# Sliding-window attention and a SwiGLU block on one core: the order of the first loads, and where two-chunk blocks begin

## Chip, cores, metric

The kernel runs on one core of one Trainium2 chip. The metric is device microseconds (us) of one execution. The median of three runs before the change is 333.36 us (332.61 to 333.39).

## What is computed

Attention with a causal window of 64 positions over 8 batches, 8 heads, 576 positions and head size 64, and then a gated feed-forward over all 4608 tokens:

```python
scores = scale * np.matmul(q, k.transpose(0, 1, 3, 2))
mask = (rel >= 0) & (rel < window)                 # rel = query - key, window = 64
attn = softmax(np.where(mask, scores, -1e9))
x = np.matmul(attn, v)                             # tokens x 512 after the heads are joined
g = x @ w_gate
val = x @ w_val
out = (g * sigmoid(g) * val) @ w_out               # 512 -> 1536 -> 512
```

All inputs and the output are float32 in memory; the kernel computes in bfloat16 and accumulates in float32.

## The kernel before

**Tiling.** The 4608 tokens are 36 chunks of 128; four chunks are one feed-forward group of 512, so there are nine groups. A chunk goes through four steps. Its q and k are laid out transposed (qT, kT). `Sb` or `Sk` (L412, L442) makes the scores on PE, and ACT takes their exponential into pt. `AVs`, `AVmm` or `AVp` (L536, L496, L568) multiplies pt with V on PE, and DVE divides by the sum (`AVn`, `AVpn`), which gives xb. `X` (L654) transposes xb into xT, on PE with a copy by ACT or DVE, or by a DMA transpose on the SP queue. A group's feed-forward is `F` (L713): for one or two of the twelve 128-wide slices f, eight or sixteen matmuls with Wg and Wv (L733), a tanh on ACT (L739) and two DVE operations (L741, L743) that write hT; then `O` (L749) multiplies a chunk's hT with Wo in twelve matmuls (L759), ACT copies the result and issues the store.

**Order.** Everything is recorded in one hand-written order in `build` (L848), and each engine runs its own operations in that order; waits come from the reads and writes named with each operation (`_Graph`, L31). A DMA is issued by the engine whose queue it is recorded on: nearly all loads by POOL (`load`, `load2`, `load_w`, `load_wo`), transposes by SP, stores by ACT. So POOL does nothing further while its next operation waits. POOL's DMAs also use 16 semaphores in turn: the seventeenth waits for the first.

**The first four chunks** go a path of their own. `first_loads` fetches k of chunks 0 and 1 in float32, a DVE cast (L685, shown as L242) makes bfloat16 of it, and `first_T` transposes it on PE (L692). `T2` (L355) transposes k or q of two chunks on PE in sixteen small transposes (L368) with two copies, each on ACT or DVE; its source buffers ks2 and qs2 hold two stages of two chunks in turn. `Sbias` (L398) adds the mask as a large negative number with one matmul per bank (L406), from nmask, which DVE computes out of mask. `AVs` (L546) needs, beside V of its own chunk, a copy of V shifted by 64 rows, vs, which `shift` (L530) makes on DVE or POOL from two neighbouring chunks of V. `warm` (L700) issues matmuls on zeros, "dummies", whose result nobody reads.

**Later chunks.** From chunk 8 on, `load` brings q and k into rings of six buffers (kn, qn), and `T` (L345) transposes them by DMA on SP. `B(n)` (L641) does the attention of chunk n, with the scores of chunk n+1 between its two halves. From chunk P0 on `P(n)` (L626) does the attention of chunks n and n+1 as one block, with the scores of n+2 and n+3 between its halves; the loop over u (L960) calls it on even u behind an `O`. `kt` and `qt` (L376, L379) say up to which chunk the transposes are issued at n; they step up one chunk at P0 - 1.

The loads before the first feed-forward, in POOL's order (L798): q of chunks 0 and 1, k and q of chunks 2 and 3, identity and mask, V0, V1, Wg slices 0-1, V2, V3, Wv 0-1, Wg 2-3, the first shifted copy, Wv 2-3, both weights 4-5, three shifted copies, weights 6-9. V of a chunk is 128 KB in bfloat16, two slices of one weight 256 KB, a `load2` of k or q 256 KB, Wo 1536 KB in two halves.

Of the kernel before, what the change touches and what calls it, by code (L numbers as in the profile page):

```python
# [5 lines left out]
ALU = mybir.AluOpType  # L6
# [145 lines left out]
class _Kernel:  # L152
# [7 lines left out]
    NO = 4  # L160
    NST = 4
    KC = 18
    P0 = 20

    def __init__(self, nc, q, k, v, wg, wv, wo, out):
        self.nc, self.q, self.k, self.v = nc, q, k, v
# [98 lines left out]
            out=m[:, :], in_=m[:, :], compare_op=ALU.not_equal, fill=1.0, base=0,  # L265
            pattern=[[-1, 128]], channel_multiplier=1), writes=["ident"])

    def init_mask(self, part):
        g = self.g
        mm = self.mask[:, :].rearrange("p (v e q) -> p v e q", v=3, e=2)  # L270

        def sel(e_, cmp, fill, base, cm, step):
            a = mm[:, :, e_, :]
            g.op("pool", lambda e: e.affine_select(
                out=a, in_=a, compare_op=cmp, fill=fill, base=base,
                pattern=[[0, 3], [step, 64]], channel_multiplier=cm), writes=["mask"])

        if part == 0:
            sel(0, ALU.is_ge, 0.0, 0, -1, 1)
            sel(0, ALU.is_ge, 1.0, 64, -1, 1)  # L280
            return
        sel(1, ALU.is_gt, 0.0, 0, 1, -1)
        sel(1, ALU.is_ge, 0.0, 64, -1, 1)
        g.op("pool", lambda e: e.memset(mm[64:128, 1, 0, :], 0.0), writes=["mask"])
        g.op("pool", lambda e: e.memset(mm[0:64, 2, 1, :], 0.0), writes=["mask"])

    def init_nmask(self):
        self.g.op("dve", lambda e: e.tensor_scalar(
# [66 lines left out]
    def T2(self, st, x, engs):  # L355
        g = self.g
        src = (self.ks2 if x == "k" else self.qs2)[st % 2]
        dst = self.kT if x == "k" else self.qT
        z0 = (2 * st) % self.NZ
        for cc in range(2):  # L360
            bank, bk = self.bank("a")
            tb = bank[:, 0:256].bitcast(BF).rearrange("p (c j t) -> p c j t", c=2, j=2)

            def pe(e, cc=cc, tb=tb):
                for c in range(2):
                    for j in range(2):
                        for p in range(2):
                            r = e.transpose(tb[64 * p:64 * p + 64, c, j, :], src[:, 4 * cc + 2 * c + p, j, :], self.ident[:, :])  # L368
                return r

            g.op("pe", pe, reads=["ident", ("s2", x, st % 2, 0), ("s2", x, st % 2, 1)], writes=[bk])
            d = dst[:, 2 * cc:2 * cc + 2, 128 * z0:128 * z0 + 256].rearrange("p c (t j) -> p c t j", j=2)
            a = tb.rearrange("p c j t -> p c t j")
            self.copy(engs[cc], d, a, [bk], [(x + "T", z, cc) for z in (z0, z0 + 1)])

    def kt(self, n):  # L376
        return n + 3 + (n >= self.P0 - 1)

# [151 lines left out]
    def shift(self, n, r, eng):  # L530
        i = n + r - 1
        src, dst = self.va[n], self.vs[i]
        rows = slice(64 * r, 64 * r + 64)
        self.copy(eng, dst[rows, :, 0:64], src[rows, :, 0:64], [("va", n), ("va", n, 0), ("va", n, 1)], [("vs", i, r)])

    def AVs(self, st):  # L536
        n, bx, av, done = st
# [97 lines left out]
    def AV(self, n):  # L635
        st = self.AVa(n)
        self.AVmm(st, 0)
        self.AVmm(st, 1)
        self.AVn(st)
# [109 lines left out]
    def O(self, c, u):  # L749
        g = self.g  # L750
        ih = c % self.NH
        hT = self.hT[ih]
        io = (4 * c + u) % self.NO
        ost = self.ost[io]
        OB, ok = self.bank("f")

        def pe(e):
            for f in range(NF):
                r = e.matmul(OB[:, :], hT[:, f, 128 * u:128 * u + 128], self.Wo[:, f, :],  # L759
                             start=(f == 0), stop=(f == NF - 1))  # L760
            return r

        g.op("pe", pe, reads=self.hTk(ih) + [("Wo", f) for f in range(NF)], writes=[ok])
        g.op("act", lambda e: e.activation(ost[:, :], OB[:, :], ACTF.Copy), reads=[ok], writes=[("ost", io)])  # L764
        r0 = 512 * c + 128 * u
        g.op("act", lambda e: e.dma_start(self.out[r0:r0 + 128, :], ost[:, :]), reads=[("ost", io)], dma=True)
# [31 lines left out]
    def loads(self):  # L798
        self.first_loads()
        self.load2(0, "q")  # L800
        self.load2(1, "k")
        self.load2(1, "q")
        self.init()
        self.init_ident()
        self.init_mask(0)
        self.init_mask(1)
        self.load(0, "v")
        self.load(1, "v")
        self.load_w("g", 0, 2)
        self.load(2, "v")  # L810
        self.load(3, "v")
        self.load_w("v", 0, 2)
        self.load_w("g", 2, 4)
        self.shift(1, 1, "pool")
        self.load_w("v", 2, 4)
        self.W(4, 6)
        self.shift(2, 0, "pool")
        self.shift(2, 1, "pool")
        self.shift(3, 0, "pool")
        for a in range(6, 10, 2):  # L820
            self.W(a, a + 2)

    def early_loads(self):
        self.load2(2, "k")
        self.load2(2, "q")
        self.W(10, 12)
        self.load(4, "v")
        self.load(5, "v")

    def more_loads(self):  # L830
        self.load2(3, "k")
        self.load2(3, "q")
        self.load(6, "v")
        self.load(7, "v")
        self.load(8, "kq")
        self.load_wo(0, 6)
        self.load_wo(6, 12)
        self.load(9, "kq")
        self.load(10, "kq")
        self.load(8, "v")  # L840
        self.load(11, "kq")
        self.load(9, "v")
# [5 lines left out]
    def build(self):  # L848
        F, S, AV, X, T2, O = self.F, self.S, self.AV, self.X, self.T2, self.O
        self.loads()  # L850
        self.banks("a", [4, 5, 6, 7, 0, 1, 2, 3, 4, 5, 0, 1, 2, 3, 0, 1, 6, 7, 4, 5, 6, 7, 4, 5, 2, 3, 6, 7])
        self.warm(48, n=112)
        self.first_T(("dve", "act"))
        self.init_nmask()
        self.warm(2)
        s0 = self.Sa(0)
        T2(0, "q", ("act", "dve"))
        self.Sbias(s0)
        self.Sb(s0)
        T2(1, "k", ("dve", "dve"))  # L860
        s1 = self.Sa(1, True)
        self.Sb(s1)
        T2(1, "q", ("dve", "act"))
        self.early_loads()
        s2, s3 = self.Sa(2, True), self.Sa(3)
        a0, a1, a2, a3 = self.AVa(0), self.AVa(1), self.AVa(2), self.AVa(3)
        self.AVs(a0)
        self.shift(0, 1, "dve")
        self.shift(1, 0, "dve")
        self.AVn(a0)  # L870
        self.Sb(s2)
        self.AVs(a1)
        self.AVn(a1)
        self.Sbias(s3)
        X(0, "act", "a")
        self.Sb(s3)
        X(1, "dve", "a")
        self.warm(3, j=2)
        self.AVs(a2)
        self.AVn(a2)  # L880
        self.warm(2, j=2)
        self.AVs(a3)
        self.AVn(a3)
        F(0, (0, 1), 0, 256)
# [10 lines left out]
        F(0, (6,))  # L895
        T2(2, "k", ("act", "act"))
        T2(2, "q", ("act", "act"))
        F(0, (7,))
        S(4)
        F(0, (8,))  # L900
# [1 line left out]
        F(0, (9,))  # L902
        X(4, "act")
        T2(3, "k", ("act", "act"))
        F(0, (10,))
        a5 = self.AVa(5)
        self.AVmm(a5, 0)
        T2(3, "q", ("act", "act"))
        self.AVmm(a5, 1)
        self.AVn(a5)  # L910
        F(0, (11,))
        X(5, "act")
        F(1, (0, 1), 0, 128)
        S(6)
        F(1, (0, 1), 128, 256)
        F(1, (2, 3), 0, 256)
        self.B(6)
        F(1, (4, 5), 0, 256)
        X(6, "act")
        F(1, (6, 7), 0, 256)  # L920
        AV(7)
        self.load(12, "kq")
        self.load(10, "v")
        for n in range(8, 12):
            self.Tkq(n)
        O(0, 0)
        X(7, "act")
# [16 lines left out]
        X(9)  # L944
        self.Tkq(14)
        F(1, (9,))
        O(0, 2)
        F(1, (10,))
        self.B(10)
        F(1, (4, 5), 256, 512)  # L950
        F(1, (11,))
        X(10, "act")
        self.B(11)
        O(0, 3)
        X(11, "act")
        F(1, (6, 7), 256, 512)
        lk, lq = max(15, self.kt(12)), max(15, self.qt(12))
        tk, tq = 14, 14
        for c in range(2, NFC):
            for u in range(4):  # L960
                n = 4 * c + u + 4
# [90 lines left out]
```

## Time and profile before

| | us |
|---|---|
| median of three runs | 333.36 (332.61 to 333.39) |
| the profiled execution | 333.81 |
| its span, first to last instruction | 331.8 |
| PE busy | 322.5 (97%) |
| DVE busy | 202.3 (61%) |
| ACT busy | 136.0 (41%) |
| POOL busy, mostly with issuing loads | 108.5 (33%) |
| feed-forward matmuls L733, with Wg and with Wv | 111.4 + 111.2 |
| output matmuls L759 | 95.9 |

Times within the profile are us from the start of the span. A line number is that of the helper that records the operation, so all feed-forward matmuls share L733, and all copies of one helper share L242 (DVE, POOL) or L240 (ACT). The duration shown for a matmul includes the tail in which the next one already runs; what one costs in a row is the distance of the starts. An entry in brackets gives the idle time of the engine ahead of the instruction and what ended it. The chain of waits is followed back from the last instruction, at each step to what released it.

### The profile page before, as it was taken

To read this page: it belongs to the slowest core of one execution; us is meant where nothing else is said; L and a number is where in the kernel's file an instruction comes from. 1 tells how busy PE (TensorE), PEld (TensorE's weight loads), DVE (VectorE), ACT (ScalarE), POOL (GpSimd) and SP (SyncE) were. 2 spreads that over 40 slices of the span, in tenths; PEclk is the share of its full clock that TensorE was granted. 3 is DMA by queue.
4 is the path that set the end of the run, shared out by engine and by line. 5 is a ranking of instruction groups with operands and counts; after the bars stand their busy time and mean duration, and the time that the engine had idled before them with its cause. 6 is when DMAs were issued, how large, how long until landed. Compare 5 with 4: busy or idle time off the path is not lost.

```text
span 331.8 us, 8107 instructions
## 1 busy us (share of the span) xinstructions
PE 322.5 (97%) x3459; PEld 167.9 (51%) x3459; DVE 202.3 (61%) x350; ACT 136.0 (41%) x242; POOL 108.5 (33%) x140
## 2 busy tenths in 40 slices
PE   6789999989999999999999999999999999999996
PEld 5466577646544444444545454545454544444444
DVE  4658777558666666665565656565656566555510
ACT  2643763535444544444525252434343432332221
POOL 8899974353623533334542424100000000000000
PEclk9999999999999999999999999999999999999999
DMA  9999999999999999999999999961412111100012
GB/s 143 153 187 188 170 181 151 153 171 148 173 174 175 169 163 120 119 131 171 167 137 132 141 111 130 118 106 52 108 49 63 49 49 47 49 32 33 34 63 95
DMA packets 161572, 39.86 MB, mean 120 GB/s; under 512 B 148608, under 2 KB 157056, under 8 KB 161536
## 3 DMA queue, kind: packets, MB, share of 16 engines
q0 software_dynamic: 111056, 18.62, 76.4%
q1 hardware_dynamic: 45024, 11.15, 25.0%
q10 hardware_dynamic: 5456, 9.57, 8.9%
q8 instruction: 27, 0.44, 0.5%
q14 instruction: 9, 0.07, 0.1%
HBM read 37.75 MB, written 9.44 MB: 142 GB/s over the span
## 4 chain that ended last, share of the span: by engine, by line
PE 78%; DMA 10%; POOL 8%; SPq 1%; issue 1%; ACT 0%; DVE 0%; ACTq 0%; POOLq 0%
PE ps L733 46%; PE ps L759 26%; DMA kn<-in_k_dram 6%; DMA qT<-qn 3%; DMA va<-in_v_dram 2%; PE ps L594 2%; POOL va L319 1%; SPq L352 1%; POOL qs L328 1%; PE ps L519 1%; POOL Wv L334 1%; PE ps L462 1%; POOL ks L328 1%; POOL Wg L334 1%; PE ps L781 1%; POOL vs L242 1%
## 5 line engine op out<-in xcount | busy, mean ns | idle before, releaser
L741 DVE SCALAR_TENSOR_TENSOR uu<-sig,ps 128x512 bf16<-128x512 bf16 (+1 forms) x109 | 74.0, 679 | 71.3 <-ACT sig L739 71.3
L733 PE MATMUL ps<-xT,Wg 128*128 128x512 bf16 (+2 forms) x488 | 111.4, 355 | 0.0
L733 PE MATMUL ps<-xT,Wv 128*128 128x512 bf16 (+2 forms) x488 | 111.2, 355 | 0.0
L759 PE MATMUL ps<-Wo,hT 128*128 128x512 bf16 x420 | 95.9, 379 | 0.0
L739 ACT ACTIVATE sig<-ps 128x512 bf16<-128x512 f32 (+1 forms) x109 | 64.9, 596 | 69.1 <-PE ps L733 68.7
L743 DVE SCALAR_TENSOR_TENSOR hT<-uu,ps 128x512 bf16<-128x512 bf16 (+1 forms) x109 | 74.3, 682 | 3.8
L733 PEld LDWEIGHTS ps<-xT,Wv 128*128 128x128 bf16 x488 | 47.1, 98 | 46.4
L733 PEld LDWEIGHTS ps<-xT,Wg 128*128 128x128 bf16 x488 | 44.7, 98 | 41.9
L759 PEld LDWEIGHTS ps<-Wo,hT 128*128 128x128 bf16 x420 | 40.9, 98 | 49.0
L764 ACT ACTIVATE ost<-ps 128x512 f32<-128x512 f32 x35 | 20.9, 597 | 94.9 <-PE ps L759 94.9
L319 POOL DMA_DIRECT2D kn<-in_k_dram x31 | 27.5, 900 | 59.0 <-DMA kT<-kn 57.9
L319 POOL DMA_DIRECT2D va<-in_v_dram x40 | 35.0, 890 | 11.2 <-PE ps L594 5.9
L319 POOL DMA_DIRECT2D qn<-in_q_dram x31 | 27.6, 892 | 30.5 <-DMA qT<-qn 29.9
L438 ACT ACTIVATE pt<-ps 128x512 bf16<-128x512 f32 x36 | 19.5, 595 | 9.8 <-PE ps L430 9.8
L474 ACT ACTIVATE pt<-ps 128x512 bf16<-128x512 f32 x36 | 18.8, 601 | 5.1 <-PE ps L466 4.7
L621 DVE RECIPROCAL rp<-ps 128x14 f32<-128x14 f32 (+1 forms) x16 | 3.2, 203 | 20.5 <-PE ps L594 20.5
L482 DVE TENSOR_TENSOR pt<-pt,kmask 128x1024 bf16<-128x1024 bf16 x18 | 12.3, 684 | 3.5 <-ACT pt L474 3.5
L565 DVE TENSOR_TENSOR xb<-ps,rc 128x512 bf16<-128x512 f32 x20 | 13.8, 692 | 0.7
L482 DVE TENSOR_TENSOR pt<-pt,mask 128x1024 bf16<-128x1024 bf16 x14 | 9.6, 684 | 4.7 <-ACT pt L438 4.6
L623 DVE TENSOR_TENSOR xb<-ps,rp 128x896 bf16<-128x896 f32 (+1 forms) x16 | 11.1, 691 | 0.6
L519 PE MATMUL ps<-va,pt 64*64 64x65 bf16 x504 | 10.2, 197 | 0.1
L519 PEld LDWEIGHTS ps<-va,pt 64*64 64x64 bf16 x504 | 6.8, 106 | 5.9 <-issue 4.0
(63 smaller groups left out, 152.0 us busy)
## 6 DMA issues: line engine op xcount, KB each, us to landing
out_dram<-ost ACTq DMA_DIRECT2D x35, 256.0 KB, 3.4
va<-in_v_dram POOLq DMA_DIRECT2D x32, 128.0 KB, 7.0
kn<-in_k_dram POOLq DMA_DIRECT2D x25, 128.0 KB, 9.5
qn<-in_q_dram POOLq DMA_DIRECT2D x25, 128.0 KB, 9.5
Wg<-in_moe_w_gate_dram POOLq DMA_DIRECT2D x6, 256.0 KB, 6.5
Wv<-in_moe_w_val_dram POOLq DMA_DIRECT2D x6, 256.0 KB, 6.7
Wo<-in_moe_w_out_dram POOLq DMA_DIRECT2D x2, 768.0 KB, 16.0
qs<-in_q_dram POOLq DMA_DIRECT2D x3, 256.0 KB, 6.5
```

The lines of the kernel that those rows point to most:

```text
L319: self.g.op("pool", lambda e, d=d, a=a: e.dma_start(d, a), writes=ks, dma=True)
L438: g.op("act", lambda e, po=po, p=p: e.activation(po, sv[p], ACTF.Exp, scale=SCALE), reads=[bx[p][1]], writes=[pk[p]])
L474: g.op("act", lambda e, po=po, p=p: e.activation(po, sv[p], ACTF.Exp, scale=SCALE), reads=[bx[p][1]], writes=[pk[p]])
L482: self.g.op("dve", lambda e: e.tensor_tensor(pt, pt, m, ALU.mult), reads=pk + [key], writes=pk)
L519: x = e.matmul(av[64 * c:64 * c + 64, p, j, :], pp[rows, h, 64 * a:64 * a + 64], vv[rows, h, 0:65], start=first, stop=phase == 1, skip_gro ...
L565: g.op("dve", lambda e: e.tensor_tensor(xo, av[:, :, :, 0:64], rb, ALU.mult), reads=bk + [("rc", ir)], writes=[("xb", ix, 0), ("xb", ix, 1)])
L733: r = e.matmul(bank[:, a * n:a * n + n], W[:, kk, f * 128:f * 128 + 128], xT[:, kk, lo:hi], start=(kk == 0), stop=(kk == NK - 1))
L739: g.op("act", lambda e, G=bank: e.activation(sig[:, 0:w], G[:, 0:w], ACTF.Tanh, scale=0.5), reads=[bk], writes=[("sig", i)])
L741: g.op("dve", lambda e: e.scalar_tensor_tensor(uu[:, 0:w], sig[:, 0:w], 1.0, G[:, 0:w], ALU.add, ALU.mult), reads=[("sig", i), gk], writes ...
L743: g.op("dve", lambda e: e.scalar_tensor_tensor(out, v3(uu), 0.5, v3(V), ALU.mult, ALU.mult), reads=[("uu", i), vk], writes=[("hT", ih, f) ...
L759: r = e.matmul(OB[:, :], hT[:, f, 128 * u:128 * u + 128], self.Wo[:, f, :], start=(f == 0), stop=(f == NF - 1))
L764: g.op("act", lambda e: e.activation(ost[:, :], OB[:, :], ACTF.Copy), reads=[ok], writes=[("ost", io)])
```

## The change

- The mask: POOL makes one half with two selects; DVE makes the other half as one minus the first and clears two corners. nmask follows at once, ahead of `first_T`.
- POOL's order: V0 to V3 directly behind the mask, then Wg and Wv 0-1, Wg 2-3, the first shifted copy (chunk 0, moved from DVE to POOL), Wv 2-3, Wg 4-5, four shifted copies, Wv 4-5, weights 6-7. Weights 8-9 now follow k and q of chunks 4 and 5.
- The scores of chunk 1 come ahead of `T2` of chunks 2 and 3; one copy of `T2(1, "k")` and the copy of X(0) change engines; the bias of chunk 2 is added later. Dummies: 44 of 132 columns instead of 48 of 112 at the start, and three of 512 columns instead of seven afterwards, at other places.
- k and q of chunks 8 and 9 come by `load2(4)`, in `late_loads` behind `T2` of chunks 4 and 5, and are transposed on PE by two more `T2`; the four DMA transposes go. Wo follows `load2(4)`.
- Groups 0 and 1: the attention of chunk 5 is no longer split around `T2(3, "q")`, that of chunk 7 is split around `T2(4, "q")`; F(1, (0, 1)) is one piece of 256 columns instead of two of 128; O(0, 2), F(1, (11,)), X(11) and O(0, 3) move by a step.
- P0 is 16 instead of 20: blocks of two chunks from chunk 16.

```diff
-    P0 = 20
+    P0 = 16
...
-    def init_mask(self, part):
+    def init_mask(self):
...
+        a, b = mm[:, :, 0, :], mm[:, :, 1, :]
+        for fill, base in ((0.0, 0), (1.0, 64)):
+            g.op("pool", lambda e, fill=fill, base=base: e.affine_select(
+                out=a, in_=a, compare_op=ALU.is_ge, fill=fill, base=base,
+                pattern=[[0, 3], [1, 64]], channel_multiplier=-1), writes=["mask"])
+        src = mm[:, 0:1, 0, :].to_broadcast([128, 3, 64])
+        one = g.op("dve", lambda e: e.tensor_scalar(b, src, -1.0, 1.0, ALU.mult, ALU.add), reads=["mask"], writes=["mask"])
+        g.op("dve", lambda e: e.memset(mm[64:128, 1, 0, :], 0.0), writes=["mask"])
+        g.op("dve", lambda e: e.memset(mm[0:64, 2, 1, :], 0.0), writes=["mask"], after=one)
...
+        rd = [("va", n), ("va", n, 0), ("va", n, 1)] + (["mask"] if eng == "pool" else [])
+        self.copy(eng, dst[rows, :, 0:64], src[rows, :, 0:64], rd, [("vs", i, r)])
...
+        self.init_mask()
+        self.init_nmask()
+        for n in range(4):
+            self.load(n, "v")
+        self.W(0, 2)
         self.load_w("g", 2, 4)
+        self.shift(0, 1, "pool")
+        self.load_w("v", 2, 4)
+        self.load_w("g", 4, 6)
         self.shift(1, 1, "pool")
-        self.load_w("v", 2, 4)
-        self.W(4, 6)
         self.shift(2, 0, "pool")
         self.shift(2, 1, "pool")
         self.shift(3, 0, "pool")
-        for a in range(6, 10, 2):
-            self.W(a, a + 2)
+        self.load_w("v", 4, 6)
+        self.W(6, 8)
...
         self.load2(2, "q")
+        self.W(8, 10)
         self.W(10, 12)
...
-        self.load(8, "kq")
+
+    def late_loads(self):
+        self.load2(4, "k")
+        self.load2(4, "q")
         self.load_wo(0, 6)
         self.load_wo(6, 12)
-        self.load(9, "kq")
...
-        self.warm(48, n=112)
+        self.warm(44, n=132)
         self.first_T(("dve", "act"))
-        self.init_nmask()
-        self.warm(2)
         s0 = self.Sa(0)
         T2(0, "q", ("act", "dve"))
         self.Sbias(s0)
+        self.warm(2)
         self.Sb(s0)
-        T2(1, "k", ("dve", "dve"))
         s1 = self.Sa(1, True)
         self.Sb(s1)
+        T2(1, "k", ("dve", "act"))
         T2(1, "q", ("dve", "act"))
         self.early_loads()
-        s2, s3 = self.Sa(2, True), self.Sa(3)
+        s2, s3 = self.Sa(2), self.Sa(3)
...
         self.AVs(a0)
-        self.shift(0, 1, "dve")
         self.shift(1, 0, "dve")
         self.AVn(a0)
+        self.Sbias(s2)
         self.Sb(s2)
...
-        X(0, "act", "a")
         self.Sb(s3)
+        X(0, "dve", "a")
         X(1, "dve", "a")
-        self.warm(3, j=2)
+        self.warm(1, j=2)
         self.AVs(a2)
         self.AVn(a2)
-        self.warm(2, j=2)
...
         T2(2, "q", ("act", "act"))
+        self.late_loads()
...
+        AV(5)
         F(0, (10,))
-        a5 = self.AVa(5)
-        self.AVmm(a5, 0)
+        X(5, "act")
         T2(3, "q", ("act", "act"))
-        self.AVmm(a5, 1)
-        self.AVn(a5)
         F(0, (11,))
-        X(5, "act")
-        F(1, (0, 1), 0, 128)
         S(6)
-        F(1, (0, 1), 128, 256)
+        F(1, (0, 1), 0, 256)
...
         X(6, "act")
+        T2(4, "k", ("act", "act"))
         F(1, (6, 7), 0, 256)
-        AV(7)
+        a7 = self.AVa(7)
+        self.AVmm(a7, 0)
+        T2(4, "q", ("act", "act"))
+        self.AVmm(a7, 1)
+        self.AVn(a7)
...
-        for n in range(8, 12):
+        for n in range(10, 12):
             self.Tkq(n)
...
-        O(0, 2)
         F(1, (10,))
         self.B(10)
+        O(0, 2)
         F(1, (4, 5), 256, 512)
-        F(1, (11,))
         X(10, "act")
         self.B(11)
+        F(1, (11,))
+        X(11, "act")
         O(0, 3)
-        X(11, "act")
```

More of the change, by code (lines that the diff above doesn't have):

```diff
@@ L266, in init_ident @@
             pattern=[[-1, 128]], channel_multiplier=1), writes=["ident"])
-    def init_mask(self, part):
+    def init_mask(self):
         g = self.g
         mm = self.mask[:, :].rearrange("p (v e q) -> p v e q", v=3, e=2)
[L272 to L285, printed above, removed]
+        a, b = mm[:, :, 0, :], mm[:, :, 1, :]
[7 more added lines that the diff above has]
+        g.op("dve", lambda e: e.memset(mm[0:64, 2, 1, :], 0.0), writes=["mask"], after=one)
     def init_nmask(self):
@@ L533, in shift @@
         rows = slice(64 * r, 64 * r + 64)
-        self.copy(eng, dst[rows, :, 0:64], src[rows, :, 0:64], [("va", n), ("va", n, 0), ("va", n, 1)], [("vs", i, r)])
+        rd = [("va", n), ("va", n, 0), ("va", n, 1)] + (["mask"] if eng == "pool" else [])
+        self.copy(eng, dst[rows, :, 0:64], src[rows, :, 0:64], rd, [("vs", i, r)])
     def AVs(self, st):
@@ L804, in loads @@
         self.init_ident()
[L805 to L812, printed above, removed]
+        self.init_mask()
[3 more added lines that the diff above has]
+        self.W(0, 2)
         self.load_w("g", 2, 4)
+        self.shift(0, 1, "pool")
+        self.load_w("v", 2, 4)
+        self.load_w("g", 4, 6)
         self.shift(1, 1, "pool")
-        self.load_w("v", 2, 4)
-        self.W(4, 6)
         self.shift(2, 0, "pool")
@@ L850, in build @@
         self.loads()
-        self.banks("a", [4, 5, 6, 7, 0, 1, 2, 3, 4, 5, 0, 1, 2, 3, 0, 1, 6, 7, 4, 5, 6, 7, 4, 5, 2, 3, 6, 7])
-        self.warm(48, n=112)
+        self.banks("a", [4, 5, 6, 7, 0, 1, 2, 3, 4, 5, 0, 1, 2, 3, 4, 5, 6, 7, 0, 1, 2, 3, 4, 5, 6, 7, 6, 7])
+        self.warm(44, n=132)
         self.first_T(("dve", "act"))
-        self.init_nmask()
-        self.warm(2)
         s0 = self.Sa(0)
```

## The prediction

> **What bounds the kernel now.** I read the stretches first, to see where the matrix engine (PE) is not busy, then what it waited for, then the chain that ended last.
>
> ```profile
> 5.30:6.78 1.48, 0.01 (x2) 0.01 (x1) 0.69 (x1) 0.00 (x0) 1.29 (x3) 1.00 1.84 175
> 6.78:14.00 7.22, 6.00 (x152) 3.66 (x152) 4.18 (x7) 4.59 (x9) 5.92 (x9) 1.00 1.74 149
> 14.00:27.00 13.00, 11.59 (x159) 8.96 (x160) 8.59 (x19) 5.40 (x10) 12.67 (x19) 1.00 1.47 187
> ...
> 60.00:70.00 10.00, 9.12 (x163) 6.01 (x162) 7.21 (x13) 5.08 (x10) 5.53 (x7) 1.00 1.61 166
> 119.50:160.57 41.07, 41.07 (x429) 19.52 (x430) 25.30 (x42) 16.60 (x30) 17.04 (x22) 1.00 1.37 137
> ...
> PE ps L546 <- DVE vs L242: 1.3, 1, 1.3
> PE ps L546 <- POOL vs L242: 0.9, 2, 0.5
> ```
>
> A stretch row gives its length, then busy time (and instructions) of PE, PE's weight loads, DVE, ACT and POOL, the granted clock, and the DMA engines' share and GB/s. PE lacks 1.2 to 1.5 us in each of the first three stretches and 0.88 from 60 to 70, and is full later, at a granted clock of 1.00 throughout. So there are two ways to gain: start the feed-forward sooner, or give PE less to do. The two rows of waits name the loss at the start: L546, the attention of chunks 1 to 3, waits for shifted copies of V.
>
> The start, from the chain of waits (start, length, what) and then the timeline:
>
> ```profile
> 4.94 0.36 POOL mask L274
> ...
> 6.86 0.14 POOL mask L285
> 7.01 0.85 POOL va L319
> 7.86 6.26 DMA va<-in_v_dram
> ...
> 14.90 0.69 POOL Wv L334
> ...
> 18.46 0.61 POOL vs L242
> ...
> 14.48 0.22 PE L546 MATMUL ps<-vs,pt 128*64 128x65 bf16 x1 [1.25 <-DVE vs L242]
> 19.21 0.19 PE L546 MATMUL ps<-vs,pt 128*64 128x65 bf16 x1 [0.45 <-POOL vs L242]
> 19.59 1.05 PE L733 MATMUL ps<-xT,Wg 128*128 128x256 bf16 x8
> ```
>
> POOL builds the mask until 7.00 and only then issues V. Chunk 1's V lands at 14.12; its copy frees L546 at 14.48. POOL then puts three weight issues ahead of the last three copies, which end at 19.07, so chunk 3's attention starts at 19.21 and the first feed-forward matmul at 19.59.
>
> **The change part by part.**
>
> *V ahead of weights, mask on DVE.* POOL loses two of four selects and both memsets: after the second select (4.94 + 0.36 = 5.30) V of chunk 0 can be issued at about 5.35, not 7.01, 1.65 sooner. At about 0.9 each the four V are issued at 5.35, 6.25, 7.15 and 8.05, then weights g0-1 at 8.9, v0-1 at 9.7, g2-3 at 10.4. With the 6.26 of the chain V1 lands at 12.5; V3 at about 14.2, as its own time to landing was 6.1. The first three rows below are the times to landing of V0, of V2 and V3, and of the first Wv.
>
> ```profile
> DMA to landing us min/median/max: 3.7/3.7/3.7
> DMA to landing us min/median/max: 6.1/6.1/6.2
> DMA to landing us min/median/max: 6.6/6.6/6.6
> 1.30 4.00 PE L708 MATMUL ps<-wz 128*128 128x112 bf16 x48 [1.30 <-DVE wz L245]
> 9.67 1.09 ACT L438 ACTIVATE pt<-ps 128x512 bf16<-128x512 f32 x2 [0.86 <-PE ps L430]
> 12.22 0.65 DVE L242 COPY vs<-va 64x512 bf16<-64x512 bf16 x1
> 14.14 0.28 DVE L242 COPY vs<-va 64x512 bf16<-64x512 bf16 x1 [1.27 <-DMA va<-in_v_dram]
> 6.20 0.60 POOL L284 MEMSET mask<- 64x64 bf16 x1
> 6.03 0.69 DVE L242 CAST ost<-hT 128x1024 bf16<-128x1024 f32 x1 [3.32 <-DMA hT<-in_k_dram]
> 7.82 0.25 DVE L288 TENSOR_SCALAR nmask<-mask 128x384 bf16<-128x384 bf16 x1
> ```
>
> DVE now makes the other half of the mask from 5.3 on: a tensor_scalar of 128x192 (at most the 0.25 of the 128x384 nmask), two memsets of 64x64 (0.14 each, as on POOL), and nmask itself (0.25), 0.8 in all, ending near 6.1. The cast that opens all scores stood at 6.03: I charge 0.1. These copies also meet POOL: the same 64x512 copy took 0.65 at 12.22, beside a POOL weight issue, and 0.28 at 14.14; POOL's memset took 0.60 beside the cast and its twin 0.14 right after. At the least this costs the cast nothing, at the most 0.46 (0.60 - 0.14); I take 0.37 (0.65 - 0.28), about what PE and DVE get back where nmask (0.25) and two 512-column dummies no longer stand ahead of T2.
>
> [...] The rows agree that the two engines block each other. [...]
>
> PE's new order puts the scores of chunk 1 ahead of T2 of chunks 2 and 3. Half of T2(1,k) moves from DVE to ACT, behind two pairs of exponentials (1.09 a pair, now from 9.67, then from about 9.3): to 11.5, then two copies of 0.60, so chunk 2's scores start near 12.7. Then: chunk 1's attention at max(12.7 + 0.4, V1 12.5 + copy 0.65) = 13.15 instead of 14.48; chunk 3's scores and exponentials end near 15.5 (13.15 + 0.35 attention, 0.5 bias, 0.4 scores, 1.1 exponentials). POOL: copy (0,1) at 11.1 (V0 is there: it landed 3.7 after its issue), two weights, then four copies of 0.61 from 13.4 to 15.8. Behind those copies stand all later weights: this is the wait that the change adds, and it holds only if V3 is later than about 15. Chunk 3's attention is then at 15.9, the first feed-forward at 16.35. The weights v0-1, last to land of the first pair, took 6.6 from an issue at 11.2 (17.8); issued at 9.7 they come at 16.3 to 17.6, wanted 0.88 after the start. Bounds: 16.3 if all goes so, 17.6 if V3 lands no sooner than its present 16.5 (copy 0.6, attention 0.4). I take 16.8: **-2.8** (-2.0 to -3.3).
>
> The dummies: 44 x 132 against 48 x 112 columns, +432 columns; they end at 1.30 + 4.00 = 5.30 and PE idles till 6.78, so nothing, and 0.2 without that cover. The fewer 512-column dummies lay in the waits above.
>
> *PE transposes for chunks 8 and 9, and groups 0 and 1.*
>
> ```profile
> 42.85 0.64 PE L368 MATMUL ps<-ident,qs 128*64 128x128 bf16 x16
> 43.42 0.32 PE L519 MATMUL ps<-va,pt 64*64 64x65 bf16 x16
> 47.05 0.62 PE L733 MATMUL ps<-xT,Wg 128*128 128x128 bf16 x8
> ...
> 47.95 1.04 PE L733 MATMUL ps<-xT,Wg 128*128 128x256 bf16 x8
> 48.83 1.04 PE L733 MATMUL ps<-xT,Wv 128*128 128x256 bf16 x8
> ...
> 68.22 0.24 PE L426 MATMUL ps<-qT,kT 64*64 64x128 bf16 x2 [0.88 <-DMA qT<-qn]
> ...
> 35.16 18.62 DMA kn<-in_k_dram
> ...
> 58.60 9.57 DMA qT<-qn
> ```
>
> Start to start, one T2 takes 43.42 - 42.85 = 0.57; two more are **+1.15** on PE. Their four ACT copies (0.60 each) lie beside matmuls, ACT being busy 5.08 of 10 in the row of 60 to 70. Two 128-column halves take 47.95 - 47.05 = 0.90 each where one 256-column piece takes 2 x 0.88: **-0.1** (0 to -0.2). Chunk 5's attention loses its split and chunk 7's gains one: no net.
>
> In exchange the 0.88 goes. SP issues the transpose of chunk 10's q at 58.60, behind those of chunks 8 and 9; landing took 9.57. Chunk 9's k, issued at 35.16, landed 18.62 later. Chunk 10's k is issued about there after the change (rival 3), lands at 53.8, and SP, free of chunks 8 and 9, issues its k then and its q at about 55.1: landed at 64.7. PE wants it at 67.35 (68.22 less the wait) - 2.8 + 1.15 - 0.1 = 65.6. **-0.9** (0 to -0.9).
>
> *Two-chunk blocks from 16.*
>
> ```profile
> 127.38 0.25 PE ps L519 x16
> 127.30:144.41 17.11, 17.11 (x169) 8.11 (x172) 10.76 (x19) 6.95 (x12) 5.76 (x7) 1.00 1.28 117
> 159.43:176.21 16.78, 16.78 (x184) 8.06 (x188) 10.86 (x18) 6.73 (x12) 8.05 (x11) 1.00 1.66 151
> ```
>
> Two chunks one by one take 17.11 (17.03 from their first matmul, 127.38), as a block 16.78: 0.25 to 0.33 less. Two more blocks give -0.5 to -0.65; I take **-0.5**, since the row's stretch begins 0.08 ahead of the matmul. The extra scores before the first block (chunk 21, now 17) only move. Transposes for chunks 18 to 20 come together, but 15 us ahead of use, as at the present switch (144.41 to 159.43).
>
> The sum: -2.8 + 1.15 - 0.1 - 0.9 - 0.5 = **-3.15**. The profiled execution took 333.81 us (span 331.8, 2.0 around it), so 330.65; the median of the three runs, 333.36, lies 0.45 below it, and the forecast for the median is **330.2**.
>
> **The rivals.**
>
> 1. *V comes no sooner.* The issue moves, but DVE's holds and the queue in front of it leave V3 at its 16.5: the first feed-forward at 17.6, gain 2.0 instead of 2.8, 331.0. For: between 6.78 and 14.00 DMA already moved 149 GB/s, not far under the 187 after it. Against: 149 is less, and while POOL builds the mask, until 7.01, it issues no transfer, and that hole is closed.
>
> 2. *The transfers of chunk 10 set the pace anyway.* DMA moves about 170 GB/s without a gap from 14 to 70; if its last q transpose lands at 68.17 as now, everything gained before is waited away, and only the blocks (-0.5) stay: 332.9. For: 512 KB for chunks 8 and 9 now stand ahead of Wo, where 256 KB stood, and what is behind is unchanged in bytes. Against: four transposes and the hole are gone.
>
> 3. *Slower.*
>
> ```profile
> 32.78 0.61 PE L368 MATMUL ps<-ident,qs 128*64 128x128 bf16 x16
> 33.55 1.80 POOL L339 DMA_DIRECT2D Wo<-in_moe_w_out_dram  x2
> 36.90 1.07 POOL L319 DMA_DIRECT2D kn<-in_k_dram  x1
> ```
>
> The load for chunks 8 and 9 uses the buffers of chunks 4 and 5, so POOL stands at it until PE's T2 of those (now 32.8) is over, with both Wo and chunk 10 behind it. Today the first Wo is issued at 33.55 and chunk 10 at 36.9. If that wait and the extra 256 KB (1.4 at 187 GB/s) make chunk 10's transpose later by x, the time changes by x - 0.5; it is slower from x = 0.5 and by over 0.3% from 1.5. With x = 2: 334.9. Against: T2 would be over by 30 to 31 (32.78 + 0.5 - 2.8), and four issues of 0.87 and two of Wo, half of 1.80 each, end by 36, ahead of the 36.9 of now.
>
> 4. *The blocks from 16 run dry*, their transposes 18 to 20 arriving late as DMA is still at a share of 1.37 after 119.5: some 1.8 lost once, 332.0. Against: a lead of 15 us, where the slow landing of chunk 10 took 9.57.
>
> **How the numbers follow.** Forecast 0.57, rival 1 0.20, rival 2 0.09, rival 3 0.09, rival 4 0.05. The forecast's own range, from the bounds of its terms, is 329.2 to 331.5. Eight in ten hold down to 329.0 and up to 332.7, short of rivals 2 and 3. A measurement of this kernel tells about 0.3%, 1.0 us, from no change: faster is the forecast, rival 1 and most of rival 4 (0.80), the same is rival 2 and the rest (0.11), slower rival 3 (0.09).
>
> **What would show it.** First L733 matmul near 16.8; POOL's V issue at 5.35 and no wait of PE for vs above 0.6; no wait of PE for qT near 65; two more L368 groups of 16 at 0.57; blocks at L594 from about 122, 16.8 apart. Wrong would be a first L733 after 17.6, a wait of L759 for Wo, or one of L426 for qT of over 1 us.

## The result and the profile after

The changed kernel takes 331.32 us (median of 22 runs, 330.24 to 334.41), the kernel before beside it on the same chip 333.22 (22 runs, 332.18 to 334.86). The ratio is 0.9947, with an interval of 0.9929 to 0.9966: 1.9 us, or 0.53%, faster. The forecast was 330.2. The profiled execution took 331.88 us, its span 330.0. The line numbers have moved by five or six: feed-forward L728, output L754, `T2` L362, second scores L456, attention of a block L589, of the first chunks L541, `first_T` L687, dummies L703, DMA transposes L346.

The stretches that the prediction began with (columns as there):

```profile
5.30:6.78 1.48, 0.29 (x6) 0.11 (x2) 1.32 (x5) 0.00 (x0) 1.40 (x2) 1.00 1.58 154
6.78:14.00 7.22, 6.63 (x174) 4.18 (x178) 4.27 (x10) 4.98 (x10) 7.18 (x10) 1.00 2.02 171
14.00:27.00 13.00, 12.41 (x152) 9.54 (x152) 10.19 (x23) 5.43 (x11) 12.86 (x20) 1.00 1.53 192
60.00:70.00 10.00, 10.00 (x218) 6.21 (x215) 8.77 (x16) 5.17 (x10) 3.63 (x5) 1.00 1.53 160
119.50:160.57 41.07, 39.78 (x456) 19.38 (x455) 24.91 (x43) 16.42 (x31) 18.51 (x22) 1.00 1.76 155
```

PE gained 0.6 to 0.8 us in the second and third row, and the 0.88 missing from 60 to 70 are back. The last row is the surprise: PE was full there before and now lacks 1.29. Of all waits of PE from 27 us to the end, the view of waits has this one row (us in total, times, longest), and the chain of waits has its place:

```profile
PE ps L456 <- issue: 1.3, 1, 1.3
```

The chain:

```profile
119.81 2.59 PE ps L754 x12
122.40 0.40 PE ps L589 x32
...
123.08 1.29 issue
124.36 0.24 PE ps L456 x2
```

It lies inside the first two-chunk block, between its two halves, in the scores of chunk 19. The page puts it down to "issue", so it names no releaser. The timeline of the start and of the two new `T2`:

```profile
4.41 0.88 POOL L273 TENSOR_SCALAR_AFFINE_SELECT mask<-mask 128x192 bf16<-128x192 bf16 x2
5.38 3.80 POOL L313 DMA_DIRECT2D va<-in_v_dram  x4
5.85 0.49 DVE L282 TENSOR_SCALAR nmask<-mask 128x384 bf16<-128x384 bf16 x1
6.27 0.67 DVE L242 CAST ost<-hT 128x1024 bf16<-128x1024 f32 x1
...
13.47 2.61 POOL L242 COPY vs<-va 64x512 bf16<-64x512 bf16 x4
...
16.36 0.22 PE L541 MATMUL ps<-vs,pt 128*64 128x65 bf16 x1
...
16.73 1.05 PE L728 MATMUL ps<-xT,Wg 128*128 128x256 bf16 x8
...
49.71 0.64 PE L362 MATMUL ps<-ident,ks 128*64 128x128 bf16 x16
...
52.38 0.64 PE L362 MATMUL ps<-ident,qs 128*64 128x128 bf16 x16
```

V goes out at 5.38, the last shifted copies end at 13.47 + 2.61 = 16.08, and the first feed-forward matmul is at 16.73 instead of 19.59.

To see where the time is kept or lost, take the start of the same output matmuls in the timelines of four profiled executions (E1 and E3 are below):

| start of | before | after | E1, blocks from 20 | E3, transposes sooner |
|---|---|---|---|---|
| first feed-forward | 19.59 | 16.73 | 16.73 | 16.60 |
| O(0, 0) | 54.91 | 53.20 | 53.42 | 53.30 |
| O(1, 0) | 88.75 | 85.83 | 85.83 | 85.71 |
| the last group's O | 315.80 | 313.79 | 312.79 | 312.16 |

In E1 and E3 the first of the twelve matmuls of O(0, 0) has no record, so those two entries are one matmul, 0.22, too late. After leads before by 2.86, 1.71, 2.92 and 2.01. So 0.9 of a lead of 2.9 is lost behind O(1, 0), where the blocks from 16 should add to it.

The reason is on SP. Its timeline, with POOL's loads in between:

```profile
109.60 1.19 SPq L658 DMA_TRANSPOSE xT<-xb  x1
110.61 0.89 POOL L313 DMA_DIRECT2D qn<-in_q_dram  x1 [5.47 <-DMA qT<-qn]
110.83 2.63 SPq L346 DMA_TRANSPOSE kT<-kn  x2
...
113.51 2.78 SPq L346 DMA_TRANSPOSE qT<-qn  x2
...
115.40 0.88 POOL L313 DMA_DIRECT2D kn<-in_k_dram  x1 [0.39 <-DMA kT<-kn]
116.34 2.13 SPq L346 DMA_TRANSPOSE kT<-kn  x1
```

And the q transposes of that row of four, by line (start of the first and the last, then the time to landing):

```profile
L346 SPq DMA_TRANSPOSE qT<-qn x2: 1345/1370/1395, 113.5 to 114.9; - x2
...
DMA to landing us min/median/max: 8.6/9.0/9.4
```

At chunk 15 SP issues k of 18 and 19, then q of 19 and 20, behind the xT of the chunk and 1.3 to 1.4 apart. The scores of chunk 19 also read q of chunk 20. That transpose is the fourth, issued at 114.9; it lands 9.4 later, at 124.3, and PE, ready at 123.08, starts at 124.36. The lead from issue to use is 8.2 us. At its own switch, from chunk 20, the kernel before had no more (the fourth at 151.8, second scores from 159.6 to about 160.3), but there the q transposes landed fast (before, by line):

```profile
L352 SPq DMA_TRANSPOSE qT<-qn x2: 1264/1283/1302, 150.5 to 151.8; - x2
...
DMA to landing us min/median/max: 3.3/3.4/3.5
```

POOL's loads around them, from the timeline of before:

```profile
147.39 0.90 POOL L319 DMA_DIRECT2D va<-in_v_dram  x1
153.76 0.88 POOL L319 DMA_DIRECT2D kn<-in_k_dram  x1 [5.47 <-DMA kT<-kn]
```

POOL issued no load from 148.3 to 153.76 there, while the four went out; after the change it issues six loads between 110.61 and 116.28, in the same 6 us as the four transposes. Three more executions show the same four transposes with other loads beside them (E2, E4 and E9 are described below). In E2 POOL issues five loads until 117.34, the fourth transpose goes out at 117.4 and takes 9.3, and PE starts the scores of chunk 19 at 126.83. In E9 five loads end at 114.70, and the fourth, out at 114.8, takes 8.4; PE starts at 123.28. In E4 the loads end at 115.96, before either q transpose is out; the fourth, out at 118.0, takes 5.7, and PE doesn't wait. So each time PE waits, it starts when the fourth has landed. That the loads make the landing up to 2.8 times as long (9.4 against 3.3) is read from these rows; no run here keeps the transposes and takes only the loads away.

### The profile page after: what moved, and what is told of

Its sections match the earlier page's. It is cut to its first block, busy times and chain, and to the rows that moved or that the text cites. A ratio compares the mean times of both kernels' runs of the same rounds, so it can differ in the third digit from the quotient of the medians.

```text
span 330.0 us, 8110 instructions
## 1 busy us (share of the span) xinstructions
PE 321.8 (98%) x3467; PEld 168.6 (51%) x3467; DVE 201.8 (61%) x350; ACT 137.6 (42%) x245; POOL 107.2 (32%) x137
## 3 DMA queue, kind: packets, MB, share of 16 engines
q10 hardware_dynamic: 5456, 9.57, 9.1%
## 4 chain that ended last, share of the span: by engine, by line
PE 94%; ACT 2%; issue 1%; POOL 1%; DVE 1%; POOLq 0%
PE ps L728 56%; PE ps L754 28%; PE ps L589 2%; PE ps L513 2%; PE ps L456 1%; PE ps L362 1%; PE ps L420 1%; PE ps L776 1%; PE ps L665 1%; PE ps L424 1%; ACT pt L432 1%; POOL qs L322 1%; ACT kT L240 0%; ACT qT L240 0%; PE ps L541 0%
## 5 line engine op out<-in xcount | busy, mean ns | idle before, releaser
L736 DVE SCALAR_TENSOR_TENSOR uu<-sig,ps 128x512 bf16<-128x512 bf16 x108 | 73.9, 684 | 65.8 <-ACT sig L734 65.7
L728 PE MATMUL ps<-xT,Wg 128*128 128x512 bf16 (+1 forms) x480 | 111.3, 358 | 0.0
L728 PE MATMUL ps<-xT,Wv 128*128 128x512 bf16 (+1 forms) x480 | 111.0, 358 | 0.0
L754 PE MATMUL ps<-Wo,hT 128*128 128x512 bf16 x420 | 95.9, 379 | 0.0
L734 ACT ACTIVATE sig<-ps 128x512 bf16<-128x512 f32 x108 | 64.8, 600 | 70.8 <-PE ps L728 70.6
L738 DVE SCALAR_TENSOR_TENSOR hT<-uu,ps 128x512 bf16<-128x512 bf16 x108 | 74.2, 687 | 3.7
L728 PEld LDWEIGHTS ps<-xT,Wv 128*128 128x128 bf16 x480 | 47.0, 98 | 46.4
L728 PEld LDWEIGHTS ps<-xT,Wg 128*128 128x128 bf16 x480 | 44.7, 98 | 42.8
L754 PEld LDWEIGHTS ps<-Wo,hT 128*128 128x128 bf16 x420 | 40.8, 98 | 48.7
L313 POOL DMA_DIRECT2D kn<-in_k_dram x29 | 25.0, 868 | 47.6 <-DMA kT<-kn 46.9
L313 POOL DMA_DIRECT2D qn<-in_q_dram x29 | 24.9, 867 | 46.7 <-DMA qT<-qn 43.4
L618 DVE TENSOR_TENSOR xb<-ps,rp 128x896 bf16<-128x896 f32 (+1 forms) x20 | 13.8, 691 | 0.7
L560 DVE TENSOR_TENSOR xb<-ps,rc 128x512 bf16<-128x512 f32 x16 | 11.1, 692 | 0.6
L589 PEld LDWEIGHTS ps<-va,pt 64*64 64x64 bf16 x632 | 7.8, 107 | 4.4 <-issue 4.2
L589 PE MATMUL ps<-va,pt 64*64 64x65 bf16 x632 | 9.6, 194 | 0.1
```

What stands on the lines that cost most here:

```text
L313: self.g.op("pool", lambda e, d=d, a=a: e.dma_start(d, a), writes=ks, dma=True)
L589: z = e.matmul(self.psa[64 * c:64 * c + 64, o:o + 65], pt[p][rows, h, 64 * a:64 * a + 64], va[m][rows, h, 0:65], start=first, stop=phase = ...
L618: g.op("dve", lambda e, d=d, num=num, rb=rb: e.tensor_tensor(d, num, rb, ALU.mult), reads=bk + [("rp", k)], writes=xk)
L728: r = e.matmul(bank[:, a * n:a * n + n], W[:, kk, f * 128:f * 128 + 128], xT[:, kk, lo:hi], start=(kk == 0), stop=(kk == NK - 1))
L734: g.op("act", lambda e, G=bank: e.activation(sig[:, 0:w], G[:, 0:w], ACTF.Tanh, scale=0.5), reads=[bk], writes=[("sig", i)])
L736: g.op("dve", lambda e: e.scalar_tensor_tensor(uu[:, 0:w], sig[:, 0:w], 1.0, G[:, 0:w], ALU.add, ALU.mult), reads=[("sig", i), gk], writes ...
```

## The experiments

Three sets of four, each with runs of the kernel before on the same chip (medians 333.34, 333.32 and 333.34):

| | kernel | us, median (lowest to highest, runs) | ratio to before, interval |
|---|---|---|---|
| E1 | after, blocks from 20 | 331.23 (331.13 to 331.44, 6) | 0.9932 (0.9915 to 0.995) |
| E2 | before, blocks from 16 | 333.72 (332.51 to 335.52, 12) | 1.0007 (0.9984 to 1.003) |
| E3 | after, transposes one chunk sooner | 330.45 (330.2 to 330.73, 6) | 0.991 (0.9891 to 0.993) |
| E4 | after, chunks 8, 9 by DMA transpose | 331.48 (330.71 to 332.64, 6) | 0.994 (0.9919 to 0.9962) |
| E5 | E3, whole mask on POOL | 331.88 (331.79 to 332.28, 6) | 0.9958 (0.9946 to 0.997) |
| E6 | E3, V and weights in the old order | 331.93 (331.02 to 334.66, 12) | 0.9964 (0.9949 to 0.9978) |
| E7 | E3, 48 dummies of 112 | 331.34 (330.37 to 331.72, 4) | 0.9936 (0.9917 to 0.9954) |
| E8 | E3, nmask behind `first_T` | 330.65 (329.91 to 331.51, 6) | 0.9921 (0.9905 to 0.9938) |
| E9 | after, again | 331.41 (330.35 to 335.23, 12) | 0.996 (0.9928 to 0.9992) |
| E10 | E3, again | 330.5 (330.25 to 332.45, 8) | 0.9922 (0.9895 to 0.995) |
| E11 | E3, 50 dummies of 132 | 330.82 (330.44 to 331.35, 6) | 0.9924 (0.9897 to 0.9951) |
| E12 | before, 44 dummies of 132 | 333.14 (331.86 to 334.36, 12) | 0.9997 (0.9978 to 1.0017) |

**E1 and E2: the blocks.** E1 sets `P0 = 20` in the changed kernel, E2 sets `P0 = 16` in the kernel before, and nothing else.

> The changed kernel with P0 back at 20, so chunks 16 to 19 go one by one. Theory (the wait of 1.29 us ahead of the scores of chunk 19 comes from the four transposes that P0 - 1 issues together, while loads are still landing slowly): no wait of PE for qT or at L456 over 0.3 us near 123, the blocks' saving of 0.5 is lost, the wait of 1.3 is gone, so 0.8 less than the changed kernel, ratio to the kernel before near 0.992. Rival (the wait belongs to that stretch of the run and not to the blocks: PE is now 3 us ahead of the transfers everywhere): a wait of about 1 us stays somewhere between 110 and 130, ratio 0.995 to 0.997.

> The kernel before with P0 = 16 alone. Theory: the blocks save 0.5 us of PE; PE reaches chunk 16 about 2 us later than in the changed kernel and the same four transposes stand together, so a wait of 0 to 1.3 us ahead of the scores of chunk 19 remains: between -0.5 and +0.8 us, ratio 0.9985 to 1.0025. Rival (the blocks are worth more than two windows of before show): -1 us or better with no wait, ratio 0.997.

E1 has no wait at L456. It was expected to take 0.8 less than the changed kernel: the profiled executions differ by 0.75 (331.13 against 331.88), the medians of the two sets by only 0.09. So starting the blocks four chunks earlier brings nothing as it stands. E2 shows the same without the rest of the change: its median is 0.4 above the kernel before (within the noise, by the interval), and its view of waits has the row:

```profile
PE ps L462 <- issue: 1.2, 1, 1.2
```

So the wait belongs to the blocks from 16 and not to the faster start.

**E3, E9 and E10: the wait.** E3 issues the transposes that step up at the switch one chunk sooner; E10 is E3 again, E9 the changed kernel beside it.

```diff
-        return n + 3 + (n >= self.P0 - 1)
+        return n + 3 + (n >= self.P0 - 2)
...
-        return n + 3 + (n >= self.KC - 4) + (n >= self.P0 - 1)
+        return n + 3 + (n >= self.KC - 5) + (n >= self.P0 - 2)
```

> The changed kernel with the two steps of kt and qt one chunk sooner (k at 14 instead of 15, q at 13 and 14 instead of 14 and 15), so that the transposes of chunks 18 to 20 are spread and the last q of the first block is issued second, not fourth, behind X(15). Theory: chunk 20's q lands by 121 and the wait at L456 falls from 1.29 to under 0.3 us; 1.0 to 1.3 us less than the changed kernel, ratio to the kernel before near 0.991. Rival (landing is slow because of the loads, not because of the queue on SP): the wait stays at 0.8 us or more, ratio 0.994 to 0.996.

> The changed kernel itself again, beside the one with transposes one chunk sooner (E10) on one chip. If the wait of 1.29 us for the transpose of chunk 20 is a fixed cost of the change, it appears again at L456 in this profile (1.0 to 1.5 us), and this kernel is 0.7 to 1.2 us above E10. If the wait was chance in one execution, it is below 0.3 us here and the two medians agree within 0.4 us.

> The kernel of E3 again. If sending the transposes one chunk sooner removes the wait, there is no wait for an issue at L456 here, and the time is 330.2 to 330.7, 0.7 to 1.2 us under E9. If E3 was a lucky one, it is within 0.4 us of E9.

The two halves of the first block's attention, in the timeline of the changed kernel:

```profile
122.33 0.47 PE L589 MATMUL ps<-va,pt 64*64 64x65 bf16 x32
...
124.58 0.48 PE L589 MATMUL ps<-va,pt 64*64 64x65 bf16 x32
```

The same in E9:

```profile
122.22 0.47 PE L589 MATMUL ps<-va,pt 64*64 64x65 bf16 x32
...
123.28 0.24 PE L456 MATMUL ps<-qT,kT 64*64 64x128 bf16 x2 [0.33 <-issue]
...
123.50 0.48 PE L589 MATMUL ps<-va,pt 64*64 64x65 bf16 x32
```

And in E3:

```profile
122.21 0.47 PE L589 MATMUL ps<-va,pt 64*64 64x65 bf16 x32
122.97 0.48 PE L589 MATMUL ps<-va,pt 64*64 64x65 bf16 x32
```

From half to half it is 2.25, 1.28 and 0.76 us: against E3 the block loses 1.49 in the first execution and 0.52 in E9, where the q transposes landed in 8.3 to 8.4. In E3 q of chunk 20 is issued second instead of fourth, at 112.1, and that k and q landed in 4.1 to 4.9. But POOL issues no load there from 110.0 to 113.77, so E3 changes both the lead and the loads beside the transposes, and the cause that its rival names (the loads make the landing slow) isn't refuted. E3's kernel is 0.9 us under the changed one, on one chip (330.5 in E10 against 331.41 in E9, though the intervals of their ratios overlap) as between the sets (330.45 against 331.32). The wait comes in both profiles of the changed kernel and in E2; its size changes from run to run, and E9's 0.33 is below what was expected. The blocks without the wait bring 0.78 by the medians of E1 and E3. E3 is the fastest version here.

**E4: transposes on PE for chunks 8 and 9.**

```diff
-        self.load2(4, "k")
-        self.load2(4, "q")
+        self.load(8, "kq")
         self.load_wo(0, 6)
         self.load_wo(6, 12)
+        self.load(9, "kq")
...
-        T2(4, "k", ("act", "act"))
...
-        T2(4, "q", ("act", "act"))
...
-        for n in range(10, 12):
+        for n in range(8, 12):
```

> The changed kernel with q and k of chunks 8 and 9 loaded and transposed by DMA again, as before, and without the two T2. Theory (the transfers of chunk 10 bound PE): PE saves 1.14 us and meets a wait for qT of 2 to 3 us at the scores of chunk 10 near 65, so 0.5 to 2 us more than the changed kernel, ratio 0.996 to 1.001. Rival (the hole closed at the start was enough): wait for qT under 1 us, the time falls by up to 1.1 us, ratio 0.991 to 0.994.

Its timeline has two waits where the kernel before had one of 0.88:

```profile
62.31 0.24 PE L420 MATMUL ps<-qT,kT 64*64 64x128 bf16 x2 [2.06 <-DMA qT<-qn]
...
67.79 0.24 PE L420 MATMUL ps<-qT,kT 64*64 64x128 bf16 x2 [1.08 <-DMA qT<-qn]
```

A faster start without the PE transposes only waits longer for the DMA transposes: 3.14 instead of 0.88. At the first block, which PE reaches at 124.89, there is no wait. The lead isn't longer there: the fourth transpose goes out at 118.0, 7.4 ahead of its reader at 125.43, but it lands in 5.7. With that wait gone, E4's median is only 0.16 above the changed kernel, where at least 0.5 was expected. Against E3, which has neither wait, it is 1.0 above. The profiled execution is the longest of its six, so 3.14 is above the usual.

**E5 and E6: the two halves of the faster start.** E5 puts the selects and memsets of the mask back on POOL in E3's kernel; E6 puts back the order V0, V1, Wg, V2, V3, Wv and three copies behind three more weight issues.

> The kernel of E3 (the change with the transposes spread) with the mask built on POOL by four selects and two memsets, as before. Theory (POOL's queue sets the start: everything behind the mask moves with it): V0 is issued at 7.0 instead of 5.38, the last shifted copy ends 1.6 us later, the first L728 comes at 18.2 to 18.4 instead of 16.7, and the time is 1.5 us above E3, near 332.0, ratio 0.9955. Rival (the transfers set the start, and a later V finds less queue): first L728 at most 0.7 us later, time within 0.7 of E3.

> The kernel of E3 with POOL's old order of V and weights: V0, V1, Wg 0-1, V2, V3, Wv 0-1, Wg 2-3, two copies, Wv 2-3, both weights 4-5, three copies. The mask stays on DVE. Theory (the copies wait for POOL, not for V): the last copies stand behind one more weight issue, 0.75, so the first L728 comes at 17.2 to 17.5 instead of 16.7 and the time is 0.5 to 0.8 us above E3. Rival (V ahead of the weights is what brings the start): V3 lands behind Wg 0-1, first L728 at 18 or later, 1.3 us or more above E3.

E5, timeline:

```profile
6.50 4.07 POOL L319 DMA_DIRECT2D va<-in_v_dram  x4
...
14.86 2.60 POOL L242 COPY vs<-va 64x512 bf16<-64x512 bf16 x4
...
17.60 0.19 PE L547 MATMUL ps<-vs,pt 128*64 128x65 bf16 x1 [0.86 <-POOL vs L242]
17.98 0.72 PE L734 MATMUL ps<-xT,Wg 128*128 128x256 bf16 x5
```

V goes out 1.12 later than after the change (1.62 was expected), the copies end 1.38 later (17.46 against 16.08), the first feed-forward comes 1.38 later than in E3, and the time is 1.43 longer: the step is passed on whole. E6's copies end at 16.77, 0.7 later. But its profiled execution, the longest of its twelve, had a slow PE at the start (see E7) and a granted clock of 0.74 from 15 to 20 us, so its first feed-forward, at 19.75, doesn't tell what the order costs, and its runs spread over 3.6 us. The median is 1.5 above E3, the lowest run 0.8 above E3's lowest: the old order is slower, by a size that isn't settled, and the two theories aren't separated.

**E7, E8, E11 and E12: dummies and nmask.** E7 and E11 change the one line `self.warm(44, n=132)` of E3's kernel into `self.warm(48, n=112)` and `self.warm(50, n=132)`, E12 puts `self.warm(44, n=132)` into the kernel before. E8 moves `self.init_nmask()` behind `first_T`.

> The kernel of E3 with 48 dummies of 112 columns at the start instead of 44 of 132. Both theories: nothing, since PE idles behind them until the first cast is done; first L687 and first L728 within 0.1 us of E3, time within 0.3 us of E3. [...]

> The kernel of E3 with nmask computed behind the first transposes instead of ahead of the cast. Theory (the vector operations ahead of the cast and their meeting with POOL's issues cost the start 0.24 us, cast at 6.27 instead of 6.03): cast at 6.05, chunk 3's exponentials and the first L728 0.2 us earlier, time 0.2 us under E3, near 330.2. Rival (the copies on POOL bind): first L728 unchanged within 0.05 us, no gain.

> The kernel of E3 with 50 dummies of 132 columns instead of 44. At the slow pace (5.02 us for 44, 0.114 each) they fill PE from 1.30 to 7.0, where the first transposes start. If the pace of PE in the first microseconds depends on how long it has been kept busy, the first transposes take 0.62 for eight in the profile, as in E3, and the time is E10's within 0.3 us with no run over 0.5 above the median. If the number of dummies costs by itself, the first transposes start later than 7.0 and the time rises by just that, 0 to 0.3. If the pace is chance, the first transposes are at times slow (1.03) here too.

> The kernel before with the change's dummies alone (44 of 132 columns instead of 48 of 112). If the dummies cost and bring nothing, as the prediction has it, the time is that of the kernel before within 0.4 us. If the longer row of dummies makes the pace of PE rise sooner, as E7 (48 of 112 in the kernel of E3, 0.9 slower) suggests, this is up to 0.9 us faster than before. In the kernel before the first feed-forward waits for V until 19.59 us, so most of a faster first scores should be waited away: 0 to 0.3 faster.

E7 was expected to cost nothing; its median is 0.9 above E3. It has four runs, the lowest, 330.37, at the level of E3, the highest, 331.72, the profiled one. The first instructions of PE in E3, from its timeline:

```profile
1.29 4.18 PE L703 MATMUL ps<-wz 128*128 128x132 bf16 x44 [1.29 <-DVE wz L245]
7.00 0.62 PE L687 MATMUL ps<-ident,ost 128*128 128x128 bf16 x8 [1.52 <-DVE ost L242]
7.55 0.64 PE L362 MATMUL ps<-ident,qs 128*64 128x128 bf16 x16
```

And in E7:

```profile
1.30 4.66 PE L703 MATMUL ps<-wz 128*128 128x112 bf16 x48 [1.30 <-DVE wz L245]
7.00 1.03 PE L687 MATMUL ps<-ident,ost 128*128 128x128 bf16 x8 [1.04 <-DVE ost L242]
7.96 1.06 PE L362 MATMUL ps<-ident,qs 128*64 128x128 bf16 x16
...
17.98 0.72 PE L728 MATMUL ps<-xT,Wg 128*128 128x256 bf16 x5
```

PE works at about 0.6 of E3's pace (1.03 against 0.62 us for the eight transposes) until past 10 us, and the first feed-forward is at 17.98, not 16.60. But the dummies don't decide this. E6, with 44 of 132, has the slow transposes too:

```profile
7.00 1.03 PE L687 MATMUL ps<-ident,ost 128*128 128x128 bf16 x8 [0.68 <-DVE ost L242]
```

And E2, with 48 of 112, has the dummies of E7 to the digit and fast transposes behind them:

```profile
1.30 4.66 PE L708 MATMUL ps<-wz 128*128 128x112 bf16 x48 [1.30 <-DVE wz L245]
6.84 0.62 PE L692 MATMUL ps<-ident,ost 128*128 128x128 bf16 x8 [0.87 <-DVE ost L242]
```

So the slow pace comes with either row of dummies, and the idle time ahead of the transposes (0.68 in E6, 0.87 in E2) doesn't decide it either. In E7's profiled execution it came with a first feed-forward 1.4 later; that E7's median is above E3 because of its dummies isn't shown. In E12 the change's dummies alone bring nothing (333.14 against 333.34); in that kernel waits for vs at L546 (0.85, 0.47 and 0.45 in E12) still lie behind the first scores. E11 fills PE further (`first_T` waits 0.20, and its eight transposes take 0.62); the time is 330.82, not less than E10, with a narrower spread (0.9 against 2.2) in too few runs to settle it. E8 gains nothing either (330.65): nmask is then late for the bias, by 0.2.

## Why the prediction was right, and where it failed

Right were the sign, the range (329.0 to 332.7) and most terms; the forecast is 1.1 us too low, and 0.8 to 0.9 of that, the distance from E3 and E10 to the changed kernel, is one step.

- *V ahead of weights, mask on DVE*, taken at -2.8: the first feed-forward came at 16.73 for a predicted 16.8, -2.86. POOL's issue of V (5.38 for 5.35) and the four copies from 13.47 to 16.08 (13.4 to 15.8) went as worked out, and E5 shows that POOL's mask was what held V back. In the profile after, PE still waits up to 0.5 at scores there, and no longer for vs. So rival 1 didn't come.
- *DVE against POOL.* The cast moved by 0.24 (6.27 against 6.03) for a charge of 0.1, and `first_T` by 0.22 (7.00 against 6.78). nmask took 0.49 instead of 0.25, and the four V issues 3.80 instead of two times 1.80. In E8, where nmask comes later, it took 0.25 and the four issues 3.68. In E5, where nmask starts at 6.58 beside the V issues (from 6.50), it took 0.26 and the four issues 4.07. So between these runs nmask differs by 0.24 and the four V issues by up to 0.47 (4.07 - 3.60), where rival 1 leaves V3 at 16.5; V3 went out at 8.3 and landed 6.1 later, at 14.4. That the two engines block each other, as the prediction reads its rows, isn't shown: nmask took 0.25 beside a V issue in the kernel before too (at 7.82, the issues from 6.96 to 8.76), and a copy of vs on DVE beside a weight issue on POOL (12.03 and 12.00, after) took 0.28, where the prediction's row has 0.65.
- *Two more `T2`*, +1.15: each took 0.57, start to start with what follows (49.71 to 50.28, 52.38 to 52.95), so +1.14. O(0, 0) leads by 1.71, which is 2.86 - 1.14 within 0.01, so the 0.1 for F(1, (0, 1)) doesn't show.
- *The wait for chunk 10's q*, -0.9: gone; PE is full from 60 to 70. Up to O(1, 0) the lead grows by 1.21; 0.88 of it is this wait, the other 0.3 wasn't separated. E4 corrects the reasoning: the price of the `T2` was set against a wait of 0.88, but with the faster start that wait would have grown, to 3.14 in the profiled execution of E4. This is rival 2, kept away by the PE transposes.
- *Rival 3* didn't come: PE waits for nothing but L456 after 27 us, so neither Wo nor chunk 10 was late.
- *Two-chunk blocks from 16*, -0.5: the size is about right: E3 leads E1 by 0.12 at O(1, 0) and by 0.63 at the last O, so its blocks gain 0.51 (E10, by the same sum, 0.34), and later blocks of the changed kernel begin 16.75 apart (140.64 and 157.39). **The step that failed** is the sentence on their transposes, "15 us ahead of use, as at the present switch (144.41 to 159.43)". It counted from the start of a chunk's attention, though SP issues the transposes behind that chunk's xT and each other: the lead of the fourth is 8.2, and was about 8 at the old switch too. And it compared that lead with one slow landing of 9.57 and called it safe: with 8.2 the same comparison says late by 1.4. The wait was 1.29. The landing, too, isn't one number: the fourth took 3.3 at the old switch and 5.7 to 9.4 at the new one. This is rival 4: the block lost 1.49 and 0.52 in the two executions, for its price of 1.8. Its chance of 0.05 was too low for a wait that came in three of the four profiled executions with this switch (after, E2, E9, not E4).
- *The dummies at nothing*: right for the kernel before (E12). In the changed kernel it is open: E7 is slower by its median, but the slow pace behind it comes with both rows of dummies. The reason given, that idle time until 6.78 covers them, leaves out how fast PE runs afterwards.

With the wait out, all steps of the sum together give 330.45 and 330.5 (E3, E10) for a forecast of 330.2. The last 0.25 to 0.3 may lie in the step from the profiled execution to the median: the forecast takes off the 0.45 by which that execution was long as if it lay outside the terms. In E2, whose start is that of the kernel before, the first feed-forward came at 19.12 instead of 19.59, so that excess may be part of the waits that the first term already counts. Two executions don't settle this.

## What to carry to other kernels

The lead of a prefetch runs from the issue of the last transfer in its burst to its first reader, not from the loop step in which it is written; compare that with the slowest landing of the same kind of transfer in the profile, taken where other queues are busy too (here 9.4 beside six loads, 3.3 without). When a change makes a stage reach its data sooner, ask of every wait behind it what it grows to, as the transposes of chunks 8 and 9 would have (0.88 to 3.14). Where a gain depends on a queue, put back each half by itself (here the mask, the order, the blocks): the halves show which one the time follows.

## What was not expected of the hardware

The pace of PE in the first microseconds differs from run to run with the same instructions. The single dummies of the changed kernel, by line (shortest, median and longest in ns):

```profile
L703 PE MATMUL ps<-wz x44: 221/316/319, 1.3 to 5.4; 128*128 128x132 bf16 x44
```

Those of E7:

```profile
L703 PE MATMUL ps<-wz x48: 276/301/302, 1.3 to 5.7; 128*128 128x112 bf16 x48
```

In the first the pace rose during the dummies, which took 4.29 us; in E7 it didn't, and transposes were slow until past 10 us. The 44 dummies of 132 took 4.18 to 5.02 us in ten executions, and the next eight transposes 0.62 in seven of them, 0.77 in E8, 0.93 in E12 and 1.03 in E6. In E1 and in E6 the dummies took 5.02; the transposes behind them were fast in E1 and slow in E6. The granted clock (the column with 1.00) in the row of E7's slow stretch:

```profile
6.78:14.00 7.22, 6.83 (x128) 4.14 (x128) 3.18 (x6) 4.06 (x8) 7.18 (x10) 1.00 2.02 172
```

So at the start the durations have to be read, not the column: it says 1.00 here, where eight transposes take 1.03, and in the same row of the changed kernel, where they take 0.62. The pace ahead of the rise is about 0.6 of the later one (1.03 against 0.62 us), and the moment of the rise changes from run to run: in E3 most dummies take 316 ns until 4.3 us and 221 from there, in E7 the slow pace lasts past 10 us. What sets that moment isn't shown by any run here. A part of the spread of these kernels, up to 4.9 us between the lowest and the highest run (E9), may come from it; this wasn't shown.
